# A three-stage attention and expert kernel: later column sums, paired weight splits, scaling on GpSimd, float64 work moved to the second pass

## The chip, the cores and the metric

One Trainium2 chip, one of its cores. The core has five engines that run side by side, each through its own instruction stream in order: TensorE (PE in the profile, with its weight loads as PEld), VectorE (DVE), ScalarE (ACT), GpSimd (POOL) and SyncE (SP), which here does little but issue DMAs. They wait for each other by semaphores. The metric is device time of one execution in microseconds (us).

## The reference, cut to what matters

```python
def _attn_ref(q, k, v):                     # (4, 8, 576, 64), chunks of 64 positions
    scores = np.matmul(q_c, k_c.transpose(0, 1, 2, 4, 3)) / np.sqrt(D)
    attn = np.exp(scores - np.max(scores, axis=-1, keepdims=True))
    attn = attn / (np.sum(attn, axis=-1, keepdims=True) + 1e-09)
    return np.matmul(attn, v_c).reshape(B, H, S, D)

def _moe_ref(x, domain_probs, w1, w2):      # x (2304, 512), 4 experts, 1024 hidden
    p = domain_probs / (domain_probs.sum(-1, keepdims=True) + 1e-09)
    for e in range(E):
        out += p[:, e:e + 1] * (np.maximum(x @ w1[e], 0.0) @ w2[e])

def _moe2_ref(x, w_gate, w_val, w_out):     # 1536 hidden; the three weights are float64
    g = x @ w_gate
    return (g / (1.0 + np.exp(-g)) * (x @ w_val)) @ w_out
```

The output of each function is the input `x` of the next. Everything is to be as exact as float32.

## The kernel before, in words

**Float32 by float16 pieces.** A float32 operand is scaled by a power of two and split into a float16 high piece h and a low piece l (what is left). A product is then three matmuls, h·h, l·h and h·l, which `half_k` issues (lines 904, 905, 906). ScalarE makes h, VectorE or GpSimd makes l (`split`, lines 134 and 135).

**The scales.** A scale comes from a bound on the norm of the operand. ScalarE squares the raw tile and adds up its rows (`squares`, line 168), TensorE adds the 128 rows with a matrix of ones (`total`, line 201), VectorE turns the sum into a power of two (`scale_by_norm`, with lines 160, 174 and 148), and ScalarE multiplies the raw tile by it (`w1_scaled`, line 529; `w2_scaled`, line 792). `total` is one tiny matmul that stands in TensorE's stream at a fixed place: if the squares are late, all matmuls behind it wait.

**Products.** Tokens are taken in three passes of 768. The first layer of the experts is cut into sets of 256 hidden columns, 16 sets for one pass. A set is computed by seven products instead of eight (Strassen-Winograd): four quarters A11, A12, A21, A22 of the weights and four sums S1 to S4 of them (`w_sums`, line 539), against quarters and sums of x. The table `PRODUCTS` has their order; `product` issues one (six matmuls of 128x384), then ScalarE keeps a partial sum (`keep`, line 888) or VectorE adds one (`plus`, line 892), and `done` makes the hidden tile's pieces hh (ScalarE, line 834) and hl (VectorE, line 835). The second layer (`layer2`, lines 953, 955, 957) turns two sets' hidden tiles into y, which VectorE adds to `acc` (line 1051). Its matmuls stand between the products, 12 or 18 at a time, twice for each set.

**What sets the order.** The program is written out in order by hand. The first blocks follow a string (`FIRST_BLOCKS`), whose letters call stages of the attention and of the first weights. Behind it one loop issues one product after another; `now` counts them, and `later(d, f)` issues f behind the product that comes d products later. `prepare` works six products ahead: in the first pass (and for three sets of the second) it makes the weights' pieces (`make_w`), stores them to memory, and the later passes load them (`load_w`). Attention of the later blocks is interleaved from a list (`rest`). The three weights of the last stage are float64: 18 generators (`make_ops`) convert them on the side (`convert`, lines 578 to 592), find a scale (`column`, `total`, `scaled`), and make and store their pieces; `run_tasks` advances up to four of them by two steps behind each product, and `yield WAIT` lets one product pass. They start when `rest` is empty, in the first pass. The last stage (gate, value, output) begins at set 48.

**Names in the rows.** `waste_w` is the output of the squares that nobody reads, `total_w` the sum for the scale of a first-layer or second-layer weight, `total` and `total_wo` those of the float64 weights, `total_v` that of v, `col`, `cols` and `col_wo` the columns that are summed, `raw` a raw weight tile, `w` the pieces.

## Time and profile before

| | us |
|---|---|
| median of three runs | 1316.71 (1316.4 to 1318.38) |
| the profiled execution | 1316.42 |
| its span in the trace | 1314.3 |
| TensorE busy in it | 1195.0 |
| VectorE busy in it | 884.3 |
| ScalarE busy in it | 660.2 |
| GpSimd busy in it | 540.6 |

The profiled execution is 2.1 us longer than its span and 0.3 us under the median, so the span stands for the kernel. A wait row names the waiting instruction, the instruction that released it, the time in total, how often, and the longest. A window row has the busy time of each engine in a stretch and the TensorE clock that was granted there (1.00 is 2.4 GHz, the other level is 0.5 of it).

### The profile page before, as it was taken

What the parts mean: (1) busy time and instruction counts of PE and PEld (TensorE: products, weight loads), DVE (VectorE), ACT (ScalarE), POOL (GpSimd) and SP (SyncE); (2) the same over time, 40 slices, a digit from 0 to 9 for tenths busy, and PEclk for the clock granted to TensorE, in tenths of its full rate; (3) what the DMA queues carried; (4) which work ended last, traced back from release to release, by engine and by line L of the source; (5) the groups of instructions that cost most, each with busy time, mean ns of one, the idle gap of its engine ahead of it and who ended that gap; (6) DMA issues with size and microseconds to landing.
All of it is one profiled execution on the core that took longest, in us unless ns stands there. A gap on an engine that the chain in (4) does not pass through costs nothing.

```text
span 1314.3 us, 21379 instructions
## 1 busy us (share of the span) xinstructions
PE 1195.0 (91%) x7274; PEld 701.7 (53%) x7274; DVE 884.3 (67%) x1743; ACT 660.2 (50%) x1385; POOL 540.6 (41%) x603
## 2 busy tenths in 40 slices
PE   7788888897777989898999999999999999999998
PEld 5444444443333445444555454555566666766776
DVE  5476555545866467787875777546558876687667
ACT  6656554554655544365555445324454544453542
POOL 4324322325758357476653767400124222222221
PEclk9799899888888999899999999999999999999999
DMA  7246536428435876465766676535376645465543
GB/s 225 97 129 220 157 106 208 130 79 300 158 115 165 201 254 196 136 217 162 241 210 172 215 256 196 165 115 187 104 175 206 211 139 182 132 208 170 147 137 105
DMA packets 180430, 227.65 MB, mean 173 GB/s; under 512 B 19664, under 2 KB 135888, under 8 KB 180320
## 3 DMA queue, kind: packets, MB, share of 16 engines
q1 hardware_dynamic: 179392, 224.80, 54.9%
q10 hardware_dynamic: 896, 1.44, 0.3%
q8 instruction: 57, 0.93, 0.3%
q14 instruction: 53, 0.43, 0.1%
q0 software_dynamic: 32, 0.04, 0.0%
HBM read 166.17 MB, written 60.03 MB: 172 GB/s over the span
## 4 chain that ended last, share of the span: by engine, by line
PE 61%; DVE 17%; ACT 9%; DMA 4%; issue 4%; POOL 2%; SPq 2%; DVEq 0%; ACTq 0%; POOLq 0%
PE y L953 7%; PE y L955 7%; PE y L957 7%; PE lx L904 5%; PE lx L906 5%; PE lx L905 5%; PE ox L1022 4%; PE oz L1022 4%; PE lz L904 3%; PE lz L906 3%; PE lz L905 3%; DVE hl L835 3%; ACT hh L834 2%; DMA w<-w 2%; DVE raw L539 2%
## 5 line engine op out<-in xcount | busy, mean ns | idle before, releaser
L953 PE MATMUL y<-w,hh 128*128 128x512 f16 x576 | 230.3, 400 | 6.2 <-DVE acc L1051 3.5
L957 PE MATMUL y<-w,hl 128*128 128x512 f16 x576 | 227.8, 396 | 2.1 <-DVE hl L835 1.8
L955 PE MATMUL y<-w,hh 128*128 128x512 f16 x576 | 229.7, 399 | 0.0
L135 POOL TENSOR_TENSOR w<-raw,w 128x256 f16<-128x256 f32 (+1 forms) x156 | 127.6, 829 | 228.0 <-ACT w L134 195.1
L135 POOL TENSOR_TENSOR ol<-sg,oh 128x384 f16<-128x384 f32 x72 | 75.5, 1059 | 330.2 <-ACT oh L134 287.8
L904 PEld LDWEIGHTS <-w 128*128 128x128 f16 x1182 | 116.3, 98 | 111.0 <-issue 34.1
L905 PEld LDWEIGHTS <-w 128*128 128x128 f16 x1182 | 116.3, 98 | 86.2 <-issue 12.9
L906 PEld LDWEIGHTS <-w 128*128 128x128 f16 x1182 | 116.5, 99 | 78.4 <-issue 3.0
L834 ACT ACTIVATE hh<-sum_p 128x384 f16<-128x384 f32 x90 | 46.9, 521 | 203.9 <-DVE sum_p L892 203.9
L1051 DVE SCALAR_TENSOR_TENSOR acc<-y,pg,acc 128x512 f32<-128x512 f32 x126 | 91.7, 744 | 80.0 <-PE y L957 79.1
L953 PEld LDWEIGHTS <-hh 128*128 128x128 f16 x576 | 59.0, 102 | 88.7 <-issue 34.2
L957 PEld LDWEIGHTS <-hl 128*128 128x128 f16 x576 | 58.8, 102 | 78.5 <-issue 13.7
L835 DVE SCALAR_TENSOR_TENSOR hl<-sum_p,hh 128x384 f16<-128x384 f32 x90 | 59.6, 662 | 59.4 <-ACT hh L834 59.4
L135 POOL TENSOR_TENSOR w_made<-raw,w_made 128x256 f16<-128x256 f32 x84 | 62.5, 752 | 86.6 <-ACT w_made L134 80.4
L955 PEld LDWEIGHTS <-hh 128*128 128x128 f16 x576 | 58.6, 102 | 73.6 <-issue 17.7
L892 DVE TENSOR_TENSOR sum_p<-lx,p 128x384 f32<-128x384 f32 x81 | 44.9, 554 | 67.9 <-PE lx L906 66.0
L134 ACT ACTIVATE w<-raw 128x256 f16<-128x256 f32 (+1 forms) x156 | 67.8, 452 | 5.2 <-DVE raw L539 5.0
L134 ACT ACTIVATE oh<-sg 128x384 f16<-128x384 f32 x72 | 36.2, 521 | 61.7 <-DVE sg L853 61.3
L134 ACT ACTIVATE o<-sg 128x384 f16<-128x384 f32 x54 | 26.7, 518 | 66.1 <-DVE sg L205 66.1
L904 PE MATMUL lx<-t2h,w 128*128 128x384 f16 x162 | 53.2, 328 | 4.6 <-ACT p L888 4.4
L904 PE MATMUL lx<-t3h,w 128*128 128x384 f16 x162 | 52.8, 326 | 3.2 <-ACT u L888 1.8
L888 ACT COPY u<-lx 128x384 f32<-128x384 f32 x81 | 38.3, 472 | 34.2 <-PE lx L906 33.8
(281 smaller groups left out, 3079.2 us busy)
## 6 DMA issues: line engine op xcount, KB each, us to landing
w<-w SPq DMA_DIRECT2D x567, 128.0 KB, 3.2
w<-w SPq DMA_DIRECT2D x96, 256.0 KB, 3.5
w<-w_made SPq DMA_DIRECT2D x84, 128.0 KB, 2.9
raw<-w SPq DMA_DIRECT2D x19, 512.0 KB, 4.1
wo_t<-wo_t SPq DMA_DIRECT2D x36, 256.0 KB, 2.8
raw<-w SPq DMA_DIRECT2D x32, 256.0 KB, 3.3
sums<-x SPq DMA_DIRECT2D x40, 192.0 KB, 4.0
xt<-sums SPq DMA_DIRECT2D x40, 192.0 KB, 3.1
```

Source lines behind the costliest of these rows:

```text
L134: nc.scalar.activation(h, src, AF.Copy)
L135: (lo or nc.vector).tensor_tensor(out=l, in0=src, in1=h, op=ALU.subtract)
L834: nc.scalar.activation(h, src, AF.Relu)
L835: nc.vector.scalar_tensor_tensor(out=l, in0=src, scalar=0.0, in1=h, op0=ALU.max, op1=ALU.subtract)
L904: nc.tensor.matmul(ps, w[:, 0, c], xh[:, k], start=f, stop=False, skip_group_check=True)
L905: nc.tensor.matmul(ps, w[:, 0, c], xl[:, k], start=False, stop=False, skip_group_check=True)
L906: nc.tensor.matmul(ps, w[:, 1, c], xh[:, k], start=False, stop=e, skip_group_check=True)
L953: nc.tensor.matmul(y, hh[:, c], w[:, 0], start=(j == 0), stop=False)
L955: nc.tensor.matmul(y, hh[:, c], w[:, 1], start=False, stop=False)
L957: nc.tensor.matmul(y, hl[:, c], w[:, 0], start=False, stop=(j == 3))
L1022: nc.tensor.matmul(o, left[:, c], w[:, k, right], start=start and t % 2 == 0 and k == 0 and i == 0, stop=k == 1 and i == 2, skip_group_che ...
L1051: nc.vector.scalar_tensor_tensor(out=sum_, in0=y, scalar=p, in1=sum_, op0=ALU.mult, op1=ALU.add)
```

## The change: what it does

1. **Sums later.** The squares of a first-layer tile are taken in two halves, four and five products behind the fetch (whole at three before), their sum on TensorE at seven (five before), the scaling at nine and ten (six before). The sum of a second-layer weight moves by two products, its column by one, its scaling by two. The sum for v comes one step of the list later. The column of a float64 tile is followed by five waits instead of two.
2. **v's scale is applied elsewhere.** `sigma` multiplies when ScalarE copies the transposed attention output, and no longer enters the softmax denominator (`back` in `att_sums` before). The norms of blocks 6 and 7 leave the string of the first blocks.
3. **Lower pieces later.** From set 3 on VectorE makes hl one product later (`later(1, low)`), and ScalarE's Exp of the later attention blocks is issued one product later.
4. **Pairs.** Weights are split, stored and loaded two products at a time (`w_pair`, `PAIRS`, 128x512 instead of 128x256), from 8 tiles of double size instead of 12.
5. **Scaling on GpSimd.** `w1_scaled` and `w2_scaled` run there; the weights of sets 0 to 2 are scaled inside their split instead (`split_scaled`).
6. **Float64 work from the second pass.** The 18 generators start at set 16, five run at a time and four tiles are held, with one step behind every third product and two behind the others; x sums go first.

```diff
+PAIRS = slice(A11, A12 + 1), slice(S1, S2 + 1), slice(S3, S4 + 1), slice(A22, A22 + 1)
...
+    def total_of(cols, name, where, n=1):
...
-        nc.tensor.matmul(ps, ones, col, start=True, stop=True)
+        for i, col in enumerate(cols):
+            nc.tensor.matmul(ps, ones, col, start=i == 0, stop=i == len(cols) - 1)
...
-            nc.scalar.copy(xb, ps)
+            nc.scalar.activation(xb, ps, AF.Copy, scale=sigma[:, a : a + 1])
...
-            col = small(f"col_{n}", 1, BF16)
-            later(3, lambda: squares(r[:, 0:4].rearrange("p b f -> p (b f)"), col, f"w1_{n}"))
-            later(5, lambda: w1_scale_of(n, total(col, f"w1_{n}", (psA, "a"))))
-            later(6, lambda: w1_scaled(n))
+            col = small(f"col_{n}", 2, BF16)
+            for i in range(2):
+                later(4 + i, lambda i=i: squares(r[:, 2 * i : 2 * i + 2].rearrange("p b f -> p (b f)"), col[:, i : i + 1], f"w1_{n}_{i}"))
+                later(9 + i, lambda i=i: w1_scaled(n, slice(2 * i, 2 * i + 2)))
+            later(7, lambda: w1_scale_of(n, total_of([col[:, i : i + 1] for i in range(2)], f"w1_{n}", (psA, "a"))))
...
-        nc.scalar.activation(r, r, AF.Copy, scale=w1_scale[weights_of(n)])
+        nc.gpsimd.tensor_scalar(out=r, in0=r, scalar1=w1_scale[weights_of(n)], scalar2=None, op0=ALU.mult)
...
-        while sets64[0] == 3:
+        while sets64[0] == 4:
             yield WAIT
...
-        yield WAIT
-        yield WAIT
+        for _ in range(5):
+            yield WAIT
         scale = small(f"scale_{name}")
         scaled(scale, total(col, name, (psA, "a")))
...
-        nc.scalar.activation(r, r, AF.Copy, scale=w2_cols[G, i])
+        nc.gpsimd.tensor_scalar(out=r, in0=r, scalar1=w2_cols[G, i], scalar2=None, op0=ALU.mult)
...
-        later(d + 1, lambda: col.append(w2_col(G, BF16)))
-        later(d + 3, lambda: w2_scale_of(G, total(col[0], f"w2_{G}", (psA, "a"))))
-        later(d + 4, lambda: w2_scaled(G, 0))
-        later(d + 5, lambda: w2_scaled(G, 1))
+        later(d + 2 + slack, lambda: col.append(w2_col(G, BF16)))
+        later(d + 3 + 2 * slack, lambda: w2_scale_of(G, total(col[0], f"w2_{G}", (psA, "a"))))
+        later(d + 4 + 2 * slack, lambda: w2_scaled(G, 0))
+        later(d + 5 + 2 * slack, lambda: w2_scaled(G, 1))
...
+            def low():
+                nc.vector.scalar_tensor_tensor(out=l, in0=src, scalar=0.0, in1=h, op0=ALU.max, op1=ALU.subtract)
+
+            if n < FIRST:
+                low()
+            else:
+                later(1, low)
...
-            "y5 h5 l5 A0 A1 B0 PW CA E E D0 l4 E n6 n7 N67A g0 g1 D1 S3"
+            "y5 h5 l5 A0 A1 B0 PW CA E E D0 l4 E g0 g1 D1 S3"
...
-        RUNNING = 4
+        RUNNING = 5
...
-                    tasks += [x_sums(1)] + make64
-            if o == (NPAIRS + 2, 1):
-                tasks.insert(0, x_sums(2))
+                    running.insert(0, [x_sums(1), WAIT])
+            if o == (NPAIRS, 1):
+                tasks += make64
+            elif o == (NPAIRS + 2, 1):
+                running.insert(0, [x_sums(2), WAIT])
...
-                run_tasks(2)
+                run_tasks(1 + (now[0] % 3 > 0))
```

Where the sum of a first-layer weight stands. Before, on TensorE at set 5: behind the product with b21, with the transpose of an attention block and the second layer's matmuls behind it.

```order
L906 LDWEIGHTS w_2_1530
L906 MATMUL lw_1712<-b21h_448,w_2_1530 128x384
L201 LDWEIGHTS ones
L201 MATMUL total_w_7_1726<-col_1558,ones 128x1
L374 MATMUL xt_1737<-ident,e_1201 128x128 x4
```

After, the same sum, now two matmuls, stands behind the product with t2.

```order
L957 LDWEIGHTS w_4_1549
L957 MATMUL lx_1627<-t2h_939,w_4_1549 128x384
L213 LDWEIGHTS ones
L213 MATMUL total_w_7_1750<-col_1504,ones 128x1
L213 LDWEIGHTS ones
L213 MATMUL total_w_7_1750<-col_1504,ones 128x1
```

Between the two places stand the transpose, 18 second-layer matmuls and the products with t4 and t2; the sum has moved behind them.

The squares of that tile in ScalarE's stream before: `hh_0_1` belongs to the product two before the sum, `hh_2_0` to the one just before it; `raw<-raw` rows are scalings.

```order
L834 ACTIVATE hh_0_1_1680<-sum_u_1678 128x384
L168 ACTIVATE waste_w_7_1685,col_1558<-raw_7_1556 128x1024
L134 ACTIVATE w_6_1687<-raw_5_894 128x256
L888 COPY p_5_1697<-lx_1690 128x384
L134 ACTIVATE w_7_1709<-raw_5_894 128x256
L834 ACTIVATE hh_2_0_1721<-sum_p_5_1719 128x384
L792 ACTIVATE raw_2_0_1479<-raw_2_0_1479,col_2_0_1598 128x1024
L134 ACTIVATE w_1_1734<-raw_6_1313 128x256
```

And after:

```order
L879 ACTIVATE hh_0_1_1618<-sum_u_1616 128x384
L137 ACTIVATE w_6_1624<-raw_5_853 128x512
L939 COPY p_5_1634<-lx_1627 128x384
L171 ACTIVATE waste_w_7_0_1640,col_1504<-raw_7_1502 128x512
L879 ACTIVATE hh_2_0_1653<-sum_p_5_1651 128x384
L171 ACTIVATE waste_w_7_1_1656,col_1504<-raw_7_1502 128x512
L137 ACTIVATE w_1_1658<-raw_6_1273 128x512
L476 ACTIVATE xb_1666<-xt_1661,sigma 128x512
```

The squares moved behind the next product's rows and were halved, two splits became one, and the scaling left the stream.

GpSimd's stream at the same sets before, all of it lower pieces of weights:

```order
L135 TENSOR_TENSOR w_7_1709<-raw_5_894,w_7_1709 128x256
L135 TENSOR_TENSOR w_1_1734<-raw_6_1313,w_1_1734 128x256
L135 TENSOR_TENSOR w_2_0_1779<-raw_2_0_1479,w_2_0_1779 128x512
L135 TENSOR_TENSOR w_2_1786<-raw_6_1313,w_2_1786 128x256
L135 TENSOR_TENSOR w_2_1_1827<-raw_2_0_1479,w_2_1_1827 128x512
```

And after (`raw_2_0` and `raw_2_1` are second-layer weights, `raw_6` and `raw_7` first-layer ones):

```order
L548 TENSOR_SCALAR raw_6_1273<-raw_6_1273,s_6_1492 128x512 x2
L138 TENSOR_TENSOR w_6_1624<-raw_5_853,w_6_1624 128x512
L138 TENSOR_TENSOR w_1_1658<-raw_6_1273,w_1_1658 128x512
L837 TENSOR_SCALAR raw_2_0_1421<-raw_2_0_1421,col_2_0_1543 128x1024
L138 TENSOR_TENSOR w_3_1760<-raw_5_853,w_3_1760 128x256
L837 TENSOR_SCALAR raw_2_1_1467<-raw_2_1_1467,col_2_1_1591 128x1024
L138 TENSOR_TENSOR w_2_0_1780<-raw_2_0_1421,w_2_0_1780 128x512
```

The scalings entered GpSimd's stream between the lower pieces.

## Rows read from the trace of the kernel before

**Rows 1.** The page's head: span, then busy time and share of each engine.
```profile
span 1314.3 us, 21379 instructions
PE 1195.0 (91%) x7274; PEld 701.7 (53%) x7274; DVE 884.3 (67%) x1743; ACT 660.2 (50%) x1385; POOL 540.6 (41%) x603
```

**Rows 2.** Windows by stage: busy us (instructions) by engine, granted clock, DMA share, GB/s.
```profile
0.00:100.00 100.00, 76.45 (x558) 50.09 (x558) 57.57 (x149) 64.22 (x135) 36.77 (x61) 0.88 0.46 148
100.00:318.00 218.00, 186.26 (x1153) 103.63 (x1152) 125.99 (x296) 124.70 (x256) 73.84 (x91) 0.91 0.52 165
318.00:450.00 132.00, 99.39 (x477) 49.19 (x476) 87.14 (x150) 76.01 (x162) 86.56 (x93) 0.88 0.53 174
450.00:890.00 440.00, 420.31 (x2229) 218.59 (x2228) 303.78 (x549) 205.90 (x441) 243.79 (x263) 0.98 0.62 195
890.00:1314.30 424.30, 412.63 (x2863) 280.18 (x2861) 309.84 (x601) 189.38 (x392) 99.61 (x96) 1.00 0.53 161
```

**Rows 3.** TensorE's waits in 0 to 100 us: in total, times, longest.
```profile
PE total_w L201 <- ACT waste_w L168: 10.4, 5, 3.1
PE total_v L201 <- ACT waste_v L168: 4.8, 2, 4.4
```

**Rows 4.** TensorE's waits in 100 to 318 us.
```profile
PE total_w L201 <- ACT waste_w L168: 21.0, 9, 3.0
PE av L430 <- DVE s L160: 2.9, 3, 1.2
```

**Rows 5.** TensorE's waits in 318 to 450 us.
```profile
PE total_w L201 <- DVE cols L778: 7.1, 2, 5.7
PE total_wo L201 <- DVE col_wo L145: 7.1, 1, 7.1
PE total L201 <- DVE col L643: 5.0, 1, 5.0
PE lx L904 <- ACT p L888: 4.4, 1, 4.4
PE total_w L201 <- DVE s L160: 3.2, 1, 3.2
```

**Rows 6.** TensorE's longest wait in 450 to 890 us.
```profile
PE total L201 <- DVE col L643: 10.7, 4, 3.7
```

**Rows 7.** Timeline of one stall: start, us, engine, line, operation, [idle before <- releaser].
```profile
133.71 0.52 ACT L834 ACTIVATE hh<-sum_u 128x384 f16<-128x384 f32 x1 [2.57 <-DVE sum_u L892]
134.14 1.04 ACT L168 ACTIVATE waste_w<-raw 128x1024 f16<-128x1024 f32 x1
...
135.32 0.16 PE L201 MATMUL total_w<-col,ones 128*128 128x1 bf16 x1 [2.63 <-ACT waste_w L168]
```

**Rows 8.** Windows of 10 us: without a stall, with two, and in the float64 work.
```profile
120.00:130.00 10.00, 10.00 (x79) 6.09 (x78) 4.97 (x12) 6.27 (x14) 2.02 (x3) 1.00 0.71 230
130.00:140.00 10.00, 6.32 (x27) 2.90 (x26) 6.40 (x21) 7.08 (x16) 2.69 (x4) 0.83 0.19 66
340.00:350.00 10.00, 6.14 (x33) 3.13 (x32) 8.94 (x10) 6.26 (x14) 9.74 (x9) 1.00 0.40 126
```

**Rows 9.** Groups by form: busy us, mean ns of one, idle before it.
```profile
L792 ACT ACTIVATE raw<-raw,col 128x1024 f32<-128x1024 f32 x16 | 18.2, 1137 | 1.9 <-DVE col L788 1.9
L529 ACT ACTIVATE raw<-raw,s 128x512 f32<-128x512 f32 x6 | 4.3, 720 | 0.7 <-DVE s L174 0.7
L134 ACT ACTIVATE w<-raw 128x256 f16<-128x256 f32 x124 | 49.9, 407 | 5.2 <-DVE raw L539 5.0
L134 ACT ACTIVATE w<-raw 128x512 f16<-128x512 f32 x32 | 19.9, 625 | 0.0
L591 POOL TENSOR_TENSOR neg<-neg,raw 128x512 f32<-128x512 f32 x24 | 32.1, 1338 | 10.2 <-DVE neg L589 5.4 <-DVE square L178 4.7
```

**Rows 10.** Timeline of VectorE's weight sums, two at a time, at 131 and 346 us.
```profile
131.41 0.75 DVE L539 TENSOR_TENSOR raw<-raw 128x256 f32<-128x256 f32 x2
...
346.14 2.92 DVE L539 TENSOR_TENSOR raw<-raw 128x256 f32<-128x256 f32 x2
```

More of the change, by code (lines that the diff above doesn't have):

```diff
@@ L417, in att_norms @@
         r = slice(a, b + 1)
-        s = st_p.tile([P, b + 1 - a], F32, tag="vs", name=f"vs{a}")
-        scale_by_norm(s, total(v_cols[:, r], f"v{a}", where, b + 1 - a), 10)
-        flip(back[:, r], s)
-        if b % BLOCKS == BLOCKS - 1 and b >= BLOCKS:
+        halve(half_bits[:, r], total(v_cols[:, r], f"v{a}", where, b + 1 - a))
+        int_scale(sigma[:, r], half_bits[:, r], -1.0, 198)
+        if b >= BLOCKS and b % BLOCKS == BLOCKS - 1:
             scaled_shares(b // BLOCKS)
@@ L539, in w_sums, with w_pair, w_of, w_store @@
             (engine or nc.vector).tensor_tensor(out=r[:, o], in0=r[:, a], in1=r[:, b], op=op)
-    def w_split(r, a, name, lo=None):
-        t = w_p.tile([P, 2, 2 * P], F16, tag="w", name=f"w_{name}_{a}")
-        split(t[:, 0], t[:, 1], r[:, a], lo=lo or nc.gpsimd)
-        return t
+    def w_pair(r, some, name, scale=None):
+        src = r[:, some]
+        t = w_p.tile([P, 2, 2, 2 * P], F16, tag="w", name=f"w_{name}_{some.start}")
+        h, l = (t[:, i, : src.shape[1]] for i in range(2))
+        if scale is None:
+            split(h, l, src, lo=nc.gpsimd)
+        else:
+            split_scaled(h, l, src, scale)
+        return t, h, l
+    def w_of(n, i, t):
+        some = PAIRS[i // 2]
+        for j in range(2):
+            if i + j < NPROD:
+                wop[n, i + j] = t[:, :, PRODUCTS[i + j][1] - some.start]
+    def w_store(to, t):
+        nc.sync.dma_start(to, t)
     def make_w(n, i):
-        a = PRODUCTS[i][1]
-        t = wop[n, i] = w_split(raw1[n], a, n)
-        later(3, lambda: nc.sync.dma_start(w_d[weights_of(n)][i], t))
+        t, h, l = w_pair(raw1[n], PAIRS[i // 2], n)
+        w_of(n, i, t)
+        to, k = w_d[weights_of(n)][i // 2], h.shape[1]
+        later(3, lambda: w_store(to[:, :, :k], t[:, :, :k]))
         if i == NPROD - 1:
@@ L630, in make_set64 @@
         into = w_d[NPAIRS + 2 * q + m]
-        stores = [(PRODUCTS[i][1], into[i]) for i in range(NPROD)]
+        stores = [(some, lambda t, k, i=i: w_store(into[i][:, :, :k], t[:, :, :k])) for i, some in enumerate(PAIRS)]
         def column(r, col):
@@ L671, in make_wo_ops @@
         return make_ops(
-            wo[c : c + 2], f"wo_{g}_{k}", sums, [(places[b], wo_ops[g][b][:, k]) for b in OUT_OPS], column, scaled
+            wo[c : c + 2], f"wo_{g}_{k}", sums, stores, column, scaled
         )
@@ L1154, in w_plain @@
         def w_plain(n, some):
[L1155 to L1157 removed]
+            t, _, _ = w_pair(raw1[n], some, n, w1_scale[n])
+            for j, a in enumerate(range(4)[some]):
+                wplain[n, a] = t[:, :, j]
         def shares():
```

92 lines of the change are left out of this document (54 added, 38 removed).

## The prediction

> **What bounds the kernel now.** I read the busy shares first. TensorE is busy for 1195.0 of 1314.3 us, 91%, and no other engine above 67% [rows 1]. So the end is set by TensorE's own work, by the 119 us in which it stands still, and by its clock. The windows by stage say where [rows 2]: it is idle for 23.6 us of the first 100, 31.7 of the next 218, 32.6 of the 132 behind them, 19.7 of the 440 us of the other two passes, and 11.7 of the 424 us of the last stage. The granted clock follows the same stages: 0.88, 0.91, 0.88, 0.98, 1.00. Clock that was not granted, taken as stage length times what is missing to 1, is 12 + 19.6 + 15.8 + 8.8 + 0 = 56 us. At most 119 + 56 = 175 us can be had without taking work from TensorE, and the change takes none away.
>
> Then I read who TensorE waits for. In each stage the largest rows are one kind of instruction, the tiny sum for a scale, and what releases it is the squares on ScalarE or the column on VectorE [rows 3 to 6]. One stall shows how [rows 7]: the squares start at 134.14 because they stand behind a hidden tile that ScalarE could only make at 133.71; they take 1.04, and the sum that TensorE had reached 2.63 us earlier runs at 135.32. In the 10 us with this stall and its smaller neighbour TensorE is busy for 6.32 and the clock granted is 0.83, a third of the stretch at the lower level of 1.2 GHz; in the 10 us ahead, where it was busy throughout, 1.00 [rows 8]. So a stall is paid twice, and I price the second part by the stages' granted clock.
>
> **The change part by part.** *Sums later, pass 1* (100 to 318 us). Rows 4 hold 21.0 us in 9 stalls for the squares and 2.9 for a bank that waits behind a sum, 23.9 of the 31.7 idle us. Before, two products separated the issue of the squares from their sum, about 2 us of TensorE work: a product is six matmuls, and the nine sets' sums each waited 2.3 us on top, so the squares are ready some 4.3 us after their place. Now a sum comes two products behind the second half of the squares, and 18 second-layer matmuls of a mean 0.22 us (the whole stage has 1153 matmuls in 186 busy us at a clock of 0.91, 0.16 each, and these are the longest) and an attention step stand between, about 6 us; and the squares are shorter, half of 1.04. So 6 stands against 4, and I take all 24 us. What is late next is hl (below), and small waits of some 8 us that stay. Of the 19.6 us of clock I take 17, since what remains idle is scattered.
>
> *Sums later, with float64 work moved* (318 to 450 us). Waits on sums are 7.1 + 7.1 + 5.0 + 3.2 = 22.4 us; the 4.4 us that a product waits for ScalarE's copy `p` is none of them [rows 5]. GpSimd is busy for 86.6 of 132 us there, and VectorE for 87.1 [rows 2]; at 340 us they stand at 9.74 and 8.94 of 10 [rows 8]. The float64 generators that fill them begin only at set 16 now, and a column has five products ahead of its sum in place of two, some 6 us more against a longest wait of 7.1. I take 21 us, and 12 of 15.8 us of clock; the 4.4 us at the pass boundary stay, with the clock behind them.
>
> *Second and third pass* (450 to 890). The sums cost 10.7 us [rows 6], the longest 3.7, less than the added products: I take 10, and 4 of 8.8 us of clock. The float64 work that came out of the stage before comes in here: 18 generators over 30 sets as before, but none of it ahead of set 16. VectorE is at 69% and GpSimd at 55% here [rows 2], so I price it at nothing; TensorE's matmuls are the cover, and if VectorE fell behind it would show as waits on hl or on a sum.
>
> *The first 100 us.* The wait of up to 4.4 us on v's squares goes, since the norms of two blocks leave the string [rows 3]. The five waits on first-layer squares are 10.4 us. Two of the five sums (sets 4 and 5) now stand behind second-layer matmuls. The other three stand in a stretch where ScalarE is the late engine, and it loses work: six halves were scaled (0.720) and split in two pieces (2 x 0.407), 1.53 us, and are now one scaled split of 128x512, 0.625 [rows 9], 0.9 us less each, 5.4 in all. I take 7 of 10.4, so 11 us here, and 6 of 12 of clock.
>
> *Scaling on GpSimd.* ScalarE loses 16 scalings of 1.137 us for the second layer [rows 9] and as many for the first, 36 us off an engine that is not late in the mean but stands in front of hh. GpSimd gets 24 of 128x512 and 20 of 128x1024, 64 times 512 columns. The trace has no scaling there; the nearest row is its two-input multiply of 128x512, 1.338 us [rows 9], the upper bound; the lower is ScalarE's 0.57 for 512 (half of 1.137). That is 36 to 86 us in the first 450, of which GpSimd is now busy for 197. I take the middle, 60. It is hidden: in a set of 24.2 us (218 us over 9 stalls) GpSimd is busy for 8.2, and at the upper bound 4 x 1.338 = 5.4 us more leave it at 13.6 in a set that I shorten to 19.5. The new wait is ScalarE's split of a second-layer weight, one product behind a GpSimd scaling of up to 2.7 us: behind it in ScalarE's queue stand the copies p and u and the tile hh, for which TensorE next needs the bank two or more products and a group of second-layer matmuls later. I charge 2 us. The trace also shows what a busy GpSimd does to VectorE: two weight sums take 0.75 us at 131, and 2.92 at 346 [rows 10], with GpSimd at 9.74 of 10 around the second [rows 8]. This speaks against the move, and I charge 4 us.
>
> The Trainium skill speaks against it too: its page "GPSIMD Engine Reference", section "Engine selection", sends elementwise work to VectorE, calls GpSimd about twice as slow for two inputs, and roughly at line rate for one. No row here has a one-input operation on GpSimd; by the page the price would be near the lower bound, 36 us of hidden work, and the sum would stay as it is.
>
> *hl one product later.* VectorE now does the next product's sum ahead of hl and no longer sits idle until ScalarE has made hh. It costs nothing where hl is needed by the second layer: three products or more lie between for all but the last tile of a group, two products and nine matmuls for that one, some 4 us. Exp, sigma: the same instructions with a scale, at nothing. *Pairs:* ScalarE pays 0.625 for two that cost 0.814, about 100 times, 19 us that are hidden; fewer DMAs, hidden, as DMA is half busy in every stage. Thirteen second matmuls of `total_of` with their loads: 1 us.
>
> **Sum.** Idle: 11 + 24 + 21 + 10 = 66. Clock: 6 + 17 + 12 + 4 = 39. Costs: 2 + 4 + 1 = 7. So 1316.4 - 66 - 39 + 7 = 1218.4, **1218 us** for the profiled execution; the median of the runs is 0.3 us above it, so the forecast for the median is the same.
>
> **The rivals.** *All of it goes.* If the stalls that I leave (small ones in the first stages, the pass boundary) go as well and the costs are nothing, TensorE's floor comes near: 1316.4 - 0.8 x (119 - 12) - 0.85 x 56 = 1183. For it: ScalarE is relieved everywhere, and VectorE no longer stands behind hh. Against it: hand-placed code keeps some waits; even 890 to 1314 us, with no sums, has 12 us idle. *Half only.* The sums are late for a reason that moves with them: VectorE and GpSimd slow each other [rows 10], the column is late again in the second pass, and hl comes late at a group's start. Then the gains of passes 2 and 3 go (10 + 4) and those of 318 to 450 us halve (33 to 16), with 10 us of new waits on hl: 1218 + 14 + 17 + 10 = 1259. For it: VectorE at 66 to 69% in these stages. Against it: their waits are short next to the added products. *Slower.* GpSimd's scaling is dear. GpSimd fills a set of 24.2 us when 512 columns cost (24.2 - 8.2) / 4 = 4.0 us, three times the two-input row; then ScalarE's splits wait for it, and the pieces of the next set are late. To lose the gains of the other stages too (about 60 us, over some 13 sets 4.6 us each) it must cost 5.1; at 6 us the first pass alone would take 4 x 6 + 8.2 = 32.2 a set, 8 us more for 13 sets, 104 - 60, so 1360. Nothing near such a price stands in the trace. *Nothing changes:* the waits move elsewhere in full, 1316.
>
> **How the numbers follow.** My forecast, 1218 (1200 to 1240), 0.55; all of it, 1183 (1170 to 1200), 0.2; half, 1259 (1240 to 1285), 0.18; no change 0.02; slower 0.05. The range from 1175 to 1265 takes in the first, most of the second and most of the third. A measurement of this kernel can tell about 0.2% from no change. Faster by over that 0.93, within it 0.02, slower 0.05.
>
> **What would show it.** Right: rows of `total_w` waiting for squares all but gone, the granted clock at 0.97 or more from 100 us on, first-pass sets of about 19.5 us, the last stage unchanged at 424 us. A scaling of 128x512 on GpSimd between 0.57 and 1.34 us. Float64 sums without a wait above 2 us. Wrong: waits of TensorE on hl, or on a bank that ScalarE holds behind a scaled weight; GpSimd above 80% in the first pass; VectorE's weight sums at 1.4 us throughout.

## The result and the profile after

| | before | after |
|---|---|---|
| median of four runs, us | 1316.88 (1316.4 to 1318.38) | 1229.39 (1227.33 to 1230.81) |
| span of the profiled execution, us | 1314.3 | 1227.0 |
| mean granted clock | 0.960 | 0.982 |

The changed kernel takes 0.9333 of the time before, with a 95% interval from 0.9316 to 0.9349: 87.5 us less, where 98 were forecast. The page's head of the kernel after, to be read against [rows 1] (the last line is the granted clock in 40 slices, in tenths):

```profile
span 1227.0 us, 20554 instructions
PE 1164.1 (95%) x7287; PEld 693.4 (57%) x7287; DVE 899.2 (73%) x1738; ACT 617.5 (50%) x1263; POOL 611.0 (50%) x533
PEclk9789999999899999999999999999999999999999
```

TensorE stands still for 1227.0 - 1164.1 = 62.9 us (119.3 before), and 1227.0 x (1 - 0.982) = 22 us of clock are not granted (some 53 before by the same sum). TensorE does the same work but for 13 tiny matmuls more; its busy time fell by 30.9 us, which is about what it gained by doing more of it at the upper clock (53 - 22). GpSimd went up by 70.4 us.

To compare stages I cut every trace at the start of the same four products: the first of set 3, and the 69th, the 105th and the 311th from there (seven make a set, so these lie in sets 12, 18 and 47). The third piece, with the end of the first pass in it, is called the pass end. These are the kernel before and the kernel after, each as windows (start:end and length, busy us and instructions of TensorE, its weight loads, VectorE, ScalarE and GpSimd, granted clock, DMA share, GB/s), before the first four stages:

```profile
0.00:92.30 92.30, 69.68 (x518) 46.12 (x519) 53.09 (x140) 58.52 (x121) 34.69 (x58) 0.87 0.44 144
92.30:317.10 224.80, 192.14 (x1188) 107.08 (x1187) 129.67 (x303) 130.41 (x269) 75.92 (x93) 0.92 0.52 165
317.10:438.00 120.90, 88.29 (x416) 43.01 (x414) 82.02 (x140) 68.53 (x144) 79.24 (x83) 0.87 0.53 175
438.00:900.10 462.10, 442.40 (x2352) 230.64 (x2350) 315.95 (x571) 216.15 (x466) 251.12 (x273) 0.99 0.62 194
```

After, all five stages:

```profile
0.00:92.10 92.10, 69.35 (x518) 44.76 (x518) 54.91 (x140) 50.74 (x105) 35.06 (x46) 0.85 0.44 144
92.10:279.70 187.60, 175.26 (x1200) 103.47 (x1199) 133.91 (x295) 111.38 (x240) 132.42 (x94) 0.99 0.59 191
279.70:370.90 91.20, 80.72 (x413) 41.34 (x412) 54.43 (x98) 45.36 (x95) 73.90 (x52) 0.93 0.67 232
370.90:811.60 440.70, 435.87 (x2354) 229.03 (x2352) 350.82 (x616) 223.51 (x438) 271.00 (x247) 1.00 0.64 207
811.60:1227.00 415.40, 402.92 (x2810) 274.79 (x2807) 305.14 (x592) 186.50 (x387) 98.58 (x96) 1.00 0.51 159
```

The gain is 0.2 us in the first stage, 37.3 in sets 3 to 12, 29.7 at the pass end, 21.3 in the second and third pass, and -1.1 in the last stage. Forecast were 17, 41, 33, 14 and 0, less 7 us of costs, for stages cut a little later (100, 318, 450 and 890 us). So the total hides two errors: the first stage gave nothing, and the later passes half as much again as forecast.

How well a stage repeats can be read from kernels whose edits lie in other stages. Sets 3 to 12 take 187.3 to 188.3 us in four traces (the kernel after, and e5, e6, e7 below), the two later passes 440.1 to 441.4 in eight; the first stage takes 90.7 to 93.2 in four (after, e4, e5, e6), and the last, which nothing changes, 414.3 to 418.5 in all. Within such a spread two kernels count as equal there.

The waits of TensorE after, sets 3 to 12, against [rows 4] (waiting instruction, what released it, us in total, times, longest):

```profile
PE s L354 <- DVE s L163: 4.0, 2, 2.5
PE et L386 <- DVE half_bits L163: 2.3, 2, 1.2
PE total_w L213 <- DVE e L376: 2.2, 2, 1.1
```

No sum waits for squares any more. What is left belongs to the attention blocks. In the first stage, against [rows 3], waits of another kind have come in:

```profile
PE plx L956 <- POOL t4l L217: 4.0, 1, 4.0
PE total_w L213 <- DVE s L163: 3.5, 1, 3.5
PE total_w L213 <- ACT hh L879: 2.4, 1, 2.4
PE total_w L213 <- ACT waste_w L171: 1.8, 1, 1.8
```

At the pass end, against [rows 5], and in the two later passes, against [rows 6]:

```profile
PE y L1006 <- POOL w L138: 7.6, 3, 3.6
...
PE y L1004 <- DVE acc L1102: 1.7, 2, 1.1
```

The second layer now waits for a weight's lower piece on GpSimd, which is busy for 73.90 of the 91.20 us of that stage; the later passes have no wait above 1.1 us, where a sum for a float64 column waited up to 3.7 before. What GpSimd pays for the scalings, as groups by form of the kernel after (busy us, mean ns of one, idle time before it), against [rows 9]:

```profile
L548 POOL TENSOR_SCALAR raw<-raw,s 128x512 f32<-128x512 f32 x24 | 40.3, 1689 | 0.0
L837 POOL TENSOR_SCALAR raw<-raw,col 128x1024 f32<-128x1024 f32 x16 | 48.4, 3024 | 10.3 <-DVE col L833 5.5 <-ACT hh L879 4.8
L548 POOL TENSOR_SCALAR raw<-raw,s 128x1024 f32<-128x1024 f32 x4 | 11.7, 2934 | 4.5 <-DMA raw<-w 4.5
```

Together 100.4 us, where the forecast took 60 and bounded it at 86.

### The profile page after: what moved, and what is told of

Its sections match the earlier page's. It is cut to its first block, busy times and chain, and to the rows that moved or that the text cites. A ratio compares the mean times of both kernels' runs of the same rounds, so it can differ in the third digit from the quotient of the medians.

```text
span 1227.0 us, 20554 instructions
## 1 busy us (share of the span) xinstructions
PE 1164.1 (95%) x7287; PEld 693.4 (57%) x7287; DVE 899.2 (73%) x1738; ACT 617.5 (50%) x1263; POOL 611.0 (50%) x533
## 4 chain that ended last, share of the span: by engine, by line
PE 55%; DVE 6%; DMA 4%; POOL 2%; issue 2%; ACT 2%; SPq 1%; POOLq 0%; DVEq 0%; ACTq 0%
PE lx L955 6%; PE lx L956 6%; PE lx L957 6%; PE y L1006 6%; PE y L1008 6%; PE y L1004 6%; PE ox L1073 4%; PE oz L1073 4%; PE lz L955 3%; PE lz L957 3%; PE lz L956 3%; DMA w<-w 2%; PE lw L955 1%; PE lw L956 1%; PE lw L957 1%
## 5 line engine op out<-in xcount | busy, mean ns | idle before, releaser
L1006 PE MATMUL y<-w,hh 128*128 128x512 f16 x576 | 220.0, 382 | 7.6 <-POOL w L138 7.6
L1004 PE MATMUL y<-w,hh 128*128 128x512 f16 x576 | 220.1, 382 | 3.7 <-ACT hh L879 2.0
L1008 PE MATMUL y<-w,hl 128*128 128x512 f16 x576 | 219.9, 382 | 0.8 <-DVE hl L882 0.8
L138 POOL TENSOR_TENSOR w<-raw,w 128x512 f16<-128x512 f32 (+1 forms) x96 | 107.7, 1134 | 78.3 <-ACT w L137 52.0
L1004 PEld LDWEIGHTS <-hh 128*128 128x128 f16 x576 | 56.7, 98 | 64.5 <-ACT hh L879 2.5
L1006 PEld LDWEIGHTS <-hh 128*128 128x128 f16 x576 | 56.7, 98 | 63.2 <-issue 3.7
L138 POOL TENSOR_TENSOR w_made<-raw,w_made 128x512 f16<-128x512 f32 (+1 forms) x48 | 55.2, 1164 | 33.9 <-ACT w_made L137 31.3
L882 DVE SCALAR_TENSOR_TENSOR hl<-sum_p,hh 128x384 f16<-128x384 f32 x90 | 68.9, 765 | 2.7 <-ACT hh L879 2.3
L137 ACT ACTIVATE w<-raw 128x512 f16<-128x512 f32 (+1 forms) x96 | 55.2, 587 | 28.6 <-POOL raw L548 15.8
```

The lines of the kernel that those rows point to most:

```text
L137: nc.scalar.activation(h, src, AF.Copy)
L138: (lo or nc.vector).tensor_tensor(out=l, in0=src, in1=h, op=ALU.subtract)
L882: nc.vector.scalar_tensor_tensor(out=l, in0=src, scalar=0.0, in1=h, op0=ALU.max, op1=ALU.subtract)
L1004: nc.tensor.matmul(y, hh[:, c], w[:, 0], start=(j == 0), stop=False)
L1006: nc.tensor.matmul(y, hh[:, c], w[:, 1], start=False, stop=False)
L1008: nc.tensor.matmul(y, hl[:, c], w[:, 0], start=False, stop=(j == 3))
```

## The experiments

The stages are cut as above, in us. "Half clock" is the time at the lower clock level, twice what the granted clock lacks.

| kernel | to set 3 | sets 3 to 12 | pass end | passes 2, 3 | rest | span | half clock |
|---|---|---|---|---|---|---|---|
| before | 92.3 | 224.9 | 120.9 | 462.0 | 414.3 | 1314.3 | 106.1 |
| after | 92.1 | 187.6 | 91.2 | 440.7 | 415.4 | 1227.0 | 44.7 |
| e2_only_sums | 93.2 | 201.5 | 118.4 | 462.0 | 415.4 | 1290.5 | 80.0 |
| e10_only_hl | 92.9 | 206.2 | 117.8 | 444.3 | 414.8 | 1276.0 | 80.5 |
| e1_sums_back | 92.0 | 195.9 | 90.1 | 440.4 | 418.5 | 1236.8 | 49.5 |
| e4_hl_now | 90.7 | 192.4 | 89.0 | 461.4 | 415.4 | 1249.0 | 41.8 |
| e5_two_waits | 92.9 | 187.6 | 91.3 | 453.1 | 418.0 | 1242.8 | 54.6 |
| e6_f64_early | 93.2 | 188.3 | 115.4 | 446.1 | 415.5 | 1258.6 | 61.4 |
| e3_scale_act | 88.0 | 181.9 | 77.1 | 440.7 | 414.9 | 1202.6 | 17.7 |
| e8_w2_act | 86.6 | 182.4 | 81.2 | 440.1 | 415.4 | 1205.7 | 17.1 |
| e9_sums_back_act | 87.3 | 199.3 | 82.7 | 440.5 | 415.2 | 1225.0 | 32.0 |
| e7_l4_first | 87.0 | 187.3 | 91.0 | 440.4 | 415.7 | 1221.4 | 31.0 |
| e11_prices | 88.6 | 191.7 | 88.5 | 440.8 | 417.2 | 1226.8 | 45.7 |
| e12_act_apart | 83.0 | 180.3 | 77.1 | 441.4 | 415.5 | 1197.4 | 10.2 |

The theory of the prediction was that the place of the sums carries the gain of the first pass, and that hl and GpSimd's scaling cost and bring next to nothing. Against it stand three others: that the relief of ScalarE by GpSimd made the first pass faster; that the later hl carries a large part, since VectorE no longer stands in order behind ScalarE; and that GpSimd's scaling is paid for on the path.

**e1_sums_back: the weights' sums at their old place, in the kernel after.**

```diff
-            for i in range(2):
-                later(4 + i, lambda i=i: squares(r[:, 2 * i : 2 * i + 2]...))
-                later(9 + i, lambda i=i: w1_scaled(n, slice(2 * i, 2 * i + 2)))
-            later(7, lambda: w1_scale_of(n, total_of(...)))
+            later(3, lambda: squares(r[:, 0:4].rearrange("p b f -> p (b f)"), col, f"w1_{n}"))
+            later(5, lambda: w1_scale_of(n, total(col, f"w1_{n}", (psA, "a"))))
+            later(6, lambda: w1_scaled(n))
...
-        later(d + 2 + slack, lambda: col.append(w2_col(G, BF16)))
+        later(d + 1, lambda: col.append(w2_col(G, BF16)))
```

> The changed kernel (1229.4 us) with one part undone: the sums for first- and second-layer weights of the first pass stand at their old places again (whole squares three products behind the fetch, sum at five, scaling at six; second-layer column and sum as before). Scaling stays on GpSimd, pairs, later hl and the moved float64 work stay. Theory 1, the place of the sum made the first pass faster: between 100 and 318 us of the old trace the changed kernel gained 40 us by the times of the same products; 30 to 41 us of it come back, 1260 to 1270 us, with about 20 us of waits of total_w for squares again. Theory 2, the relief of ScalarE by GpSimd made it: at most 1236 us, few such waits.

1236.19 us, a ratio of 0.9388 (0.9300 to 0.9477; two runs, so wide), which the total does not set apart from the kernel after; the stage does. Sets 3 to 12 lose 8.3 us against the kernel after, and keep 29.0 of the 37.3. The waits on squares are back (waits of TensorE in that stage, and the stage as a window):

```profile
PE total_w L213 <- ACT waste_w L171: 14.2, 9, 2.6
...
92.00:288.00 196.00, 176.27 (x1191) 101.36 (x1190) 129.75 (x295) 110.02 (x222) 125.02 (x85) 0.99 0.57 182
```

Nine stalls as before, at 14.2 us in place of 21.0, and yet the clock is 0.99 and not 0.92. Of the 29.0 us, TensorE's idle time gives 32.7 - 19.7 = 13.0; the other 16 are busy time that shrank (192.14 to 176.27), that is clock. So the sums' place is not what most of this stage's gain hangs on, once the rest of the change is there.

**e2_only_sums: the sums' later place alone, in the kernel before** (the later second-layer steps and split too; scaling stays on ScalarE).

```diff
-            later(3, lambda: squares(r[:, 0:4].rearrange("p b f -> p (b f)"), col, f"w1_{n}"))
-            later(5, lambda: w1_scale_of(n, total(col, f"w1_{n}", (psA, "a"))))
-            later(6, lambda: w1_scaled(n))
+            for i in range(2):
+                later(4 + i, lambda i=i: squares(...))
+                later(9 + i, lambda i=i: w1_scaled(n, slice(2 * i, 2 * i + 2)))
+            later(7, lambda: w1_scale_of(n, total_of(...)))
```

> The kernel before (1316.9 us) with this one part of the change: sums, squares in halves, columns and scalings of the first pass later; scaling stays on ScalarE, nothing else changes. Theory 1 (the place of the sum): 30 to 41 us faster, 1276 to 1287 us, the waits of total_w between 100 and 318 us gone and the granted clock there at 0.97 or more. Theory 2 (relief of ScalarE): less than 12 us faster, 1305 us or more, since ScalarE still does all scalings and the squares are late again.

1296.17 us, 0.9844 (0.9739 to 0.9949; two runs, 7.5 us apart, so the size of the gain is uncertain). Alone the sums give 23.4 us in sets 3 to 12 of the faster run, less than the 30 to 41 of the first theory, with no wait on squares left there and the clock at 0.97, and nothing in the later passes. So the same edit is worth some 23 us alone and 8 where the rest has been done: it overlaps with other parts (e9_sums_back_act shows with which).

**e10_only_hl: the later hl alone, in the kernel before.**

```diff
-            nc.vector.scalar_tensor_tensor(
-                out=l, in0=src, scalar=0.0, in1=h, op0=ALU.max, op1=ALU.subtract
-            )
+            def low():
+                nc.vector.scalar_tensor_tensor(out=l, in0=src, ...)
+            if n < 3:
+                low()
+            else:
+                later(1, low)
```

> The kernel before with one part of the change: from set 3 on VectorE makes hl one product later. Undoing it in the changed kernel gave 20.7 of the 21.3 us back that sets 18 to 47 had gained, undoing the float64 columns' distance 12.4. Theory 1, hl later is enough by itself: sets 18 to 47 take 440 to 446 us (462 before), the sets of the first pass gain too, the whole is 1280 to 1298 us. Theory 2, it needs the distance of the float64 sums beside it, since the stalls have two causes and the later one ends them: 452 to 460 us, the whole 1298 to 1312 us.

1278.07 us, 0.9694 (0.9680 to 0.9709): 40 us for one deferred instruction, about twice what the sums' place gives alone. 18.7 of it lie in sets 3 to 12 and 17.7 in the later passes. VectorE's wait for hh, in the whole kernel before, and in this one:

```profile
DVE hl L835 <- ACT hh L834: 116.0, 163, 4.3
```

```profile
DVE hl L837 <- ACT hh L834: 20.0, 23, 3.9
```

116.0 us in 163 waits became 20.0 in 23. In the kernel before, VectorE's timeline shows one of these (start, us, then [idle before it and its releaser]), and below it the same place in the kernel after, where hl of the tile before runs at once:

```profile
505.74 0.55 DVE L892 TENSOR_TENSOR sum_u<-lz,u 128x384 f32<-128x384 f32 x1
506.88 0.69 DVE L835 SCALAR_TENSOR_TENSOR hl<-sum_u,hh 128x384 f16<-128x384 f32 x1 [0.59 <-ACT hh L834]
```

```profile
433.74 0.54 DVE L943 TENSOR_TENSOR sum_u<-lz,u 128x384 f32<-128x384 f32 x1
434.21 0.54 DVE L882 SCALAR_TENSOR_TENSOR hl<-sum_p,hh 128x384 f16<-128x384 f32 x1
```

An idle 0.59 us on an engine that is busy for 67% looks free; but what stands behind it in VectorE's stream, the sums of products that free banks, the columns and the softmax steps, all come later by it. TensorE's waits in the two later passes show it: before, and below that with hl alone later,

```profile
PE total L201 <- DVE col L643: 10.7, 4, 3.7
PE y L953 <- DVE acc L1051: 3.5, 2, 2.1
```

```profile
PE total L201 <- DVE col L643: 4.5, 4, 1.7
PE y L958 <- DVE acc L1056: 0.7, 1, 0.7
```

The float64 columns came sooner though nothing in their own place had changed. TensorE's idle time in these passes fell from 19.7 to 8.4 us; the rest of the 17.7 is clock. In the first pass the squares' waits did not go (15.5 us in 9 stalls in sets 3 to 12, 21.0 before), and that stage still came down by 18.7, half of it idle time (32.7 to 23.4) and half clock (0.96).

**e4_hl_now: hl back at once, in the kernel after.**

```diff
-            if n < FIRST:
+            if n >= 0:
                 low()
```

> The changed kernel with hl made at once again, in front of the next product's sum. Theory 1, making hl later is worth little since VectorE's idle time in front of it was not on the path: 1227 to 1234 us, while VectorE's idle time in front of hl goes back up from 23 to over 100 us. Theory 2, it is why the second and third pass gained 21 us where 14 were forecast: 1236 to 1245 us, with waits of sums or of y for VectorE.

1255.34 us, 0.9535 (0.9516 to 0.9554): 26 us lost, 20.7 of them in the later passes and 4.8 in sets 3 to 12. TensorE's waits in the later passes (after, the first stood at 1.7 us, the third at 0.8, and the largest on p at 0.8):

```profile
PE y L1004 <- DVE acc L1102: 8.7, 5, 2.8
PE lx L955 <- ACT p L939: 6.1, 3, 3.6
PE y L1008 <- DVE hl L882: 5.5, 6, 2.1
```

The first and the third name VectorE. The second is ScalarE's copy p, which stands in ScalarE's stream among the tiles hh; these wait for VectorE's `sum_u` for 36.7 us in that stage, against 11.8 after, so VectorE is likely behind it too, which is not shown. Nearly the whole gain of the later passes (21.3) is lost with this one edit.

**e5_two_waits: a float64 column two products ahead of its sum, in the kernel after.**

```diff
-        for _ in range(5):
+        for _ in range(2):
```

> The changed kernel with two waits between a float64 column and its sum in place of five. Theory 1, the added distance took the float64 sums' waits away: waits of total and total_wo come back, 1 to 4 us for a good part of the 18, 1237 to 1250 us. Theory 2, it was the move to the second pass, where VectorE has no weight sums and GpSimd no weights to split: no wait over 1 us, 1226 to 1233 us.

1243.18 us, 0.9441 (0.9359 to 0.9524): 14 us lost, 12.4 in the later passes, where TensorE waits again for the columns:

```profile
PE total L213 <- DVE col L680: 6.0, 5, 2.2
PE total_wo L213 <- DVE col_wo L148: 3.1, 1, 3.1
```

The added distance seems to be needed since the float64 work moved there: with two waits the later passes take 444.3 us where that work starts in the first pass (e10_only_hl) and 453.1 where it starts in the second, though these two kernels differ in other parts too.

**e6_f64_early: the float64 work in the first pass again, in the kernel after.**

```diff
+                    tasks += make64
-            if o == (NPAIRS, 1):
-                tasks += make64
-            elif o == (NPAIRS + 2, 1):
+            if o == (NPAIRS + 2, 1):
```

> The changed kernel with the float64 work beginning in the first pass again, as soon as the attention list is empty (x sums first, five waits and five generators stay). Theory 1 (the move matters): GpSimd, busy for 78.5 of 95 us at the end of the first pass already, is overfilled, second-layer pieces and weights are late, waits of y and of products on GpSimd grow by 10 to 25 us, 1240 to 1255 us. Theory 2 (only the distance of the sums matters): 1225 to 1233 us.

1258.24 us, 0.9556 (0.9468 to 0.9643): 29 us lost, 24.2 at the pass end, where GpSimd then is busy for 102.98 of 116.00 us (waits of TensorE in that stage, and the stage as a window):

```profile
PE y L1006 <- POOL w L138: 8.9, 3, 4.6
PE y L1004 <- ACT hh L879: 5.6, 2, 3.5
PE total_w L213 <- DVE cols L823: 4.5, 2, 3.6
PE lx L955 <- ACT p L939: 4.4, 3, 2.2
...
281.00:397.00 116.00, 85.86 (x420) 41.95 (x418) 87.02 (x142) 59.16 (x119) 102.98 (x74) 0.88 0.54 180
```

Late column sums come back (`cols`), and the waits on hidden tiles and on ScalarE's copies grow (2.0 and 0.9 us after). The pass end's gain of 29.7 is mostly this part's: the sums alone (e2) gave 2.5 there, hl alone 3.1.

**e3_scale_act: both scalings on ScalarE, as before the change, in the kernel after.**

```diff
-        nc.gpsimd.tensor_scalar(out=r, in0=r, scalar1=w1_scale[weights_of(n)], scalar2=None, op0=ALU.mult)
+        nc.scalar.activation(r, r, AF.Copy, scale=w1_scale[weights_of(n)])
...
-        nc.gpsimd.tensor_scalar(out=r, in0=r, scalar1=w2_cols[G, i], scalar2=None, op0=ALU.mult)
+        nc.scalar.activation(r, r, AF.Copy, scale=w2_cols[G, i])
```

> The changed kernel with all scalings of weights back on ScalarE at the new places. Theory 1, GpSimd's scaling costs more than it gives: the trace after has it at 1.57 us for 128x512 and 2.85 for 128x1024, above the bound of 1.34 for 512, and TensorE waits 7.6 us for second-layer pieces and 4.0 for a piece of x that stand behind it in GpSimd's queue. With ScalarE these 11.6 us go, with some 5 us of clock: 1212 to 1222 us. Theory 2, the sums are on time only because ScalarE is relieved: waits of total_w for squares come back, 1235 to 1255 us.

1204.73 us, 0.9160 (0.9146 to 0.9174): 25 us faster than the change. 4.1 lie in the first stage, 5.7 in sets 3 to 12, 14.1 at the pass end, where this window stands against 91.20 us with GpSimd at 73.90:

```profile
269.90:347.00 77.10, 75.83 (x413) 40.14 (x412) 51.85 (x98) 54.68 (x106) 45.23 (x37) 1.00 0.80 271
```

ScalarE takes 39.7 us for what cost GpSimd 100.4 (16 of 1.151, 24 of 0.708, 4 of 1.134), and TensorE's idle time there falls from 10.5 to 1.3 us. So the scaling on GpSimd is on the path, not beside it, and ScalarE needs no relief once the sums are late: with all the scalings on it no sum waits for squares in sets 3 to 12.

**e8_w2_act: only the second layer's scaling on ScalarE.** The edit is the second half of the one above.

> The changed kernel with the second-layer weights alone scaled on ScalarE (16 scalings of 128x1024), first-layer ones on GpSimd. Theory 1 (GpSimd's queue is late): the waits of y for second-layer pieces (7.6 us) and of a product for a piece of x (4.0) go, 1214 to 1222 us, as good as all scalings on ScalarE or better. Theory 2: ScalarE's queue is the tight one, 1229 us or more.

1209.33 us, 0.9196 (0.9181 to 0.9212): 20 of the 25 us are the second layer's. Of the pass end's 14.1 us it brings 10.0.

**e9_sums_back_act: the sums at their old place and both scalings on ScalarE,** the edits of e1_sums_back and e3_scale_act together.

> The changed kernel with the first pass's sums at their old places and all scalings of weights on ScalarE. With scaling on GpSimd, moving the sums back cost sets 3 to 12 only 8 us of the 37 that they had gained, so something else makes the squares earlier. Theory 1, the relief of ScalarE by GpSimd: without it the squares are late again, total_w waits 20 us or more, the granted clock in these sets falls under 0.95, they take 205 to 220 us, and the whole 1228 to 1245 us. Theory 2, VectorE, which no longer stands in front of hl and so makes sums, and with them hh and the squares behind it, sooner: 188 to 198 us, and the whole 1210 to 1222 us.

1230.09 us, 0.9330 (0.9314 to 0.9345), the time of the kernel after. Against e3_scale_act the old place costs 17.4 us in sets 3 to 12, where it cost 8.3 with the scaling on GpSimd. The two parts turn on each other: with the sums at their old place GpSimd's scaling gains 3.4 us in that stage (199.3 to 195.9), with the sums late it loses 5.7. The waits on squares alone do not tell why, since they are alike (nine stalls, 14.2 us with the scaling on GpSimd, 14.8 with it on ScalarE). So the sums' later place is worth 17.4 us without GpSimd's scaling and 8.3 with it: GpSimd's scaling is one of the parts that it overlaps with. Neither theory's price was met in full.

**e7_l4_first: the last lower piece of t4 ahead of the block D0, in the kernel after.**

```diff
-            "y5 h5 l5 A0 A1 B0 PW CA E E D0 l4 E g0 g1 D1 S3"
+            "y5 h5 l5 A0 A1 B0 PW CA E E l4 D0 E g0 g1 D1 S3"
```

> The changed kernel with two steps of the first blocks exchanged: GpSimd makes the lower pieces of block 4 before it scales the first second-layer weight, not behind it. Theory 1, the first 92 us gained only 0.2 us because that scaling (2.85 us) stands in front of the pieces for which TensorE waits 4.0 us: 4 us of wait go and with them 3 to 5 us of the 10.2 us at half clock, 1220 to 1224 us. Theory 2, the wait only moves to the split of the second-layer weight: 1227 to 1231 us.

The first stage falls from 92.1 to 87.0 us, and the wait of a product for t4l is gone. But TensorE's idle time there falls by 1.7 us only (22.8 to 21.0), since waits for squares grow (4.6 us, 1.8 after); the rest is the clock, 0.92 and not 0.85. What made the wait for t4l, in GpSimd's timeline of the kernel after:

```profile
53.64 2.85 POOL L837 TENSOR_SCALAR raw<-raw,col 128x1024 f32<-128x1024 f32 x1 [4.84 <-ACT hh L879]
56.47 0.66 POOL L217 TENSOR_TENSOR t4l<-x,t4h 128x256 f16<-128x256 f32 x1
```

GpSimd stood for 4.84 us ahead of a scaling, then took 2.85, and t4l, for which TensorE waited, came behind both. The whole kernel took 1223.97 us, 0.9295 (0.9269 to 0.9321), which its interval does not set apart from the kernel after; the stage does.

**e11_prices: what is dear in GpSimd's scaling, operand or operation.** The first-layer scale is left out here (a factor of 1.0 is put for it), and the second layer's is a two-input multiply with the column read over the row.

```diff
-        nc.gpsimd.tensor_scalar(out=r, in0=r, scalar1=w1_scale[weights_of(n)], scalar2=None, op0=ALU.mult)
+        nc.gpsimd.tensor_scalar(out=r, in0=r, scalar1=1.0, scalar2=None, op0=ALU.mult)
...
-        nc.gpsimd.tensor_scalar(out=r, in0=r, scalar1=w2_cols[G, i], scalar2=None, op0=ALU.mult)
+        nc.gpsimd.tensor_tensor(out=r, in0=r, in1=w2_cols[G, i].to_broadcast([P, 2 * DM]), op=ALU.mult)
```

> A price list, not a candidate: the changed kernel with first-layer weights multiplied by the number 1 on GpSimd (the scale is left out, so the output is not the reference's) and second-layer weights multiplied there by their column as a broadcast second input. In the changed kernel GpSimd takes 1.57 us for 128x512 and 2.85 for 128x1024 with the scale read from a column. Theory 1, the column operand is dear: with a number 128x512 takes 0.6 to 1.0 us. Theory 2, the operation is dear whatever its operand: 1.5 us or more with a number. The two-input form should take the price of the float64 multiply, twice 1.34 for 128x1024, 2.6 to 2.7 us.

```profile
L548 POOL TENSOR_SCALAR raw<-raw 128x512 f32<-128x512 f32 x24 | 37.0, 1552 | 0.0
L837 POOL TENSOR_TENSOR raw<-raw,col 128x1024 f32<-128x1024 f32 x16 | 32.4, 2025 | 10.2 <-DVE col L833 5.4 <-ACT hh L879 4.8
L627 POOL TENSOR_TENSOR neg<-neg,raw 128x512 f32<-128x512 f32 x24 | 33.6, 1399 | 23.9 <-DVE neg L625 13.4 <-ACT p L939 5.5 <-issue 5.0
```

A number in place of the column leaves it at 1.552 us, so the operation is what costs. The two-input form came out well under what I had expected of it: 2.025 for 128x1024, against 3.024. The time, 1228.56 us (one run), is that of the kernel after, with 19 us less work of scaling on GpSimd (81.3 us): sets 3 to 12 took 4.1 us more, the stages on either side 3.5 and 2.7 less. Why they took more was not followed up.

**e12_act_apart: both scalings on ScalarE, and the sums of sets 4 and 5 one and three products later.**

```diff
+            late = {4: 1, 5: 3}.get(n, 0)
...
-                later(9 + i, lambda i=i: w1_scaled(n, slice(2 * i, 2 * i + 2)))
-            later(7, lambda: w1_scale_of(n, total_of(...)))
+                later(9 + i + (late if n == 5 else 0), lambda i=i: w1_scaled(n, slice(2 * i, 2 * i + 2)))
+            later(7 + late, lambda: w1_scale_of(n, total_of(...)))
```

> The changed kernel with all scalings on ScalarE (1204.7 us so far) and two sums of the first blocks moved on: that of set 4 by one product, that of set 5 by three with its scaling. With scaling on ScalarE the trace shows waits of 2.9 and 3.5 us in front of them at 70 to 77 us and 6.8 us at half clock behind them. Theory 1, they stand too near to the squares like all the others: both waits go, with about 3 us of clock, 1195 to 1201 us. Theory 2, VectorE is late there whatever the place, with weight sums and x sums in its queue: the waits move to the next instructions, 1203 to 1207 us.

1200.07 us, 0.9102 (0.9088 to 0.9115): it beats both kernels, and e3_scale_act too; of the 5.2 us between the two traces 5.0 stand in the first stage:

```profile
0.00:83.00 83.00, 65.64 (x516) 43.71 (x516) 54.84 (x137) 54.30 (x109) 27.35 (x43) 0.94 0.48 159
```

The clock there is 0.94, where it was 0.85 in the kernel after.

## Why the prediction was right and wrong

**The total and the direction** were right for the reason given at its start: TensorE's stalls and the clock that goes with them were what could be had, and 56.4 us of stalls went (66 forecast), with 31 us of clock (39). The last stage was unchanged, as forecast. That the total came within 11 us is in part luck: the later hl, for which nothing was taken, is worth 26 us within the change, and GpSimd's scaling, for which 6 were charged, costs about 25. The two largely cancel.

**Sets 3 to 12: 41 forecast, 37.3 measured.** The waits on squares went as forecast, and the clock rose to 0.99. But the whole was put down to the sums' place, which alone gives 23.4 us (e2) and whose undoing costs 8.3 (e1) to 17.4 (e9). The parts overlap: sums 23.4 and hl 18.7 alone make 42.1, more than the whole, while with GpSimd's scaling in place undoing the one costs 8.3 and undoing the other 4.8 (e4). The size was right, its cause only in part. Sets, forecast at 19.5 us, took 187.6 / (68 / 7) = 19.3; that they fit is chance, since the 24.2 us for a set before was the stage divided by its nine stalls, and by its products a set took 224.9 / (68 / 7) = 23.2.

**Pass end: 33 forecast, 29.7 measured.** Right that the float64 work held this stage up (e6: 24.2 us), though only part of that is late sums. A new wait of 7.6 us on GpSimd's pieces took part of it back, and the clock stayed at 0.93, where 0.97 had been named.

**"hl one product later ... costs nothing": the step that failed.** It was costed as a risk for TensorE's second layer, and found hidden, which holds (0.8 us of waits on hl in the later passes). What it gives was put at nothing: the prediction says that VectorE no longer sits idle until hh is there, but the 116.0 us of that idle time, on view in the waits of VectorE, have no term in the sum. Its worth is 40 us alone, 26 within the change, and without it 20.7 of the 21.3 us of passes 2 and 3 go (e4). The sum took 10 + 4 there for the added distance of the float64 sums; but their largest wait fell from 10.7 to 4.5 us with hl alone later and that distance as before (e10). The five waits do matter (12.4 us, e5), probably as the price of moving the float64 work in, which had been put at nothing.

**GpSimd's scaling: bounds and cover both failed.** The upper bound, a two-input row of 1.338 us for 128x512, was no upper bound: the scaling takes 1.689 in the mean, and with 100.4 us in all it is above the 86. And "it is hidden" was argued by the mean of a set; it holds badly where GpSimd is nearest to full, at the pass end, and where a piece is awaited at once, in the first blocks. There the sign that was named for a wrong forecast, GpSimd above 80%, did appear (73.90 of 91.20 us). Charged were 2 + 4 us; the price is 25. The Trainium skill's page "GPSIMD Engine Reference", section "Engine selection", expects one input at roughly line rate. Here one input took longer than two on the same engine (1.552 against 1.399 for 128x512, both in e11_prices), so the measurement decides against that. The page's advice against elementwise work on GpSimd, given in the Trainium skill's same section, held: with the scaling on ScalarE the kernel is 25 us faster.

**The first 92 us: 17 forecast, 0.2 measured.** TensorE's idle time did not fall at all (22.6 us before, 22.8 after). The wait on v went and that on squares fell from 10.4 us to 1.8, as forecast. But t4l behind GpSimd's scaling (4.0) and sums of weights behind work of VectorE and ScalarE (3.5 and 2.4) took their place, and the clock stayed low (0.87 before, 0.85 after). With the scaling on ScalarE the stage is 4.1 us shorter than after, with the sums of sets 4 and 5 moved as well 9.1 (e12).

**The rivals.** "All of it" was not reached by this change; e12_act_apart, at 1200, lies at its edge, so most of what it counted on was there to be had. "Half only" fell, as the columns are not late again in the second pass. "Slower" named the right mechanism, a dear scaling, at a price that would have had to be three times as high.

What stays open is how the 25 us divide between GpSimd's own queue and what a busy GpSimd does to VectorE; no run here keeps the one without the other. The pairs, the scale of v and the later Exp were not run apart: in sets 3 to 12 all parts but the sums' place and GpSimd's scaling give 25.6 us (e9), hl alone 18.7 (e10), and what makes the other 6.9 is not shown.

## What to carry over

Price the waits of the engines that TensorE waits for, not only TensorE's own: an instruction that stands in order for another engine's result delays all that is queued behind it, and issuing it one step later was worth 40 us here, alone. Before work goes to an engine that looks half idle, look at the stage where it is fullest and at who needs its next result, and take a price for the very operation. Several edits that free the same path are not worth their sum, so cost each alone and each in place.

## What was not expected of the hardware

- GpSimd multiplies a 128x512 float32 tile by a number or a column in 1.55 to 1.69 us, and 128x1024 in 2.85 to 3.02, more than its two-input multiply needs (1.34 to 1.40 for 128x512; 2.03 for 128x1024 with the column read over the row). ScalarE does the same in 0.71 and 1.15.
- VectorE's weight sums of 128x256 take longer beside a busier GpSimd. As groups by form, in the kernel after and, below it, in e3_scale_act:

```profile
L558 DVE TENSOR_TENSOR raw<-raw 128x256 f32<-128x256 f32 x64 | 46.0, 739 | 7.0 <-POOL raw L548 6.5
```

```profile
L558 DVE TENSOR_TENSOR raw<-raw 128x256 f32<-128x256 f32 x64 | 34.4, 558 | 0.5
```

  The same 64 sums, with two inputs each, cost 739 ns in the mean against 558. The mean does not follow GpSimd's work in all: it is 696 in the kernel before and 588 with hl alone later (e10), with GpSimd busy for 540.6 and 545.9 us. The Trainium skill's page "SBUF — State Buffer", section "SBUF: two separate sides", says that VectorE and GpSimd share one pair of ports, that an operation of VectorE with two inputs from SBUF competes for it with one of GpSimd's that reads SBUF, and that the loser waits out the other's whole instruction. The means of 739 and 558 agree with it; no run here shows the ports themselves.
- The same number of stalls leaves the clock at very different levels: nine of 14.2 us in all at 0.99 (e1_sums_back), nine of 15.5 at 0.96 (e10_only_hl), nine of 21.0 at 0.92 (before), all in sets 3 to 12, where TensorE's whole idle time is 19.7, 23.4 and 32.7 us. So a stall is not always paid twice, as the prediction had it; in e1_sums_back the nine were paid nearly once. What makes the difference is not shown: its stalls are hardly shorter than those of e10_only_hl (1.6 and 1.7 us in the mean).
